# Attention in a fused kernel: two units of one kind per turn of the loop

## The chip, the core and the metric

The kernel runs on one core of a Trainium2 chip. The metric is the time of one execution on the device in microseconds, lower is better. The engines named below are TensorE (PE, with its weight loads as PEld), VectorE (DVE), ScalarE (ACT), GpSimd (POOL) and SyncE (SP, which here only issues DMAs). Each engine works through its own list of instructions in order and waits on semaphores for results of the others.

## The reference

Four batches, eight heads, 576 positions, 64 features per head; 2304 tokens of 512 features; float32 in and out.

```python
scores = scale * q @ k.T                          # per batch and head, 576 x 576
rel = pos[:, None] - pos[None, :]
mask = (rel >= 0) & (rel < 32)                    # heads 0 to 3 (local)
mask = (rel >= 0) & same remainder modulo 32      # heads 4 to 7 (strided)
attn = softmax(where(mask, scores, -1e9)) @ v
x = attn as [2304, 512]
e = argmax(x @ w_gate + modality_bias[modality_id], 1)    # one of 8 experts per token
x = gate * (relu(x @ w1[e]) @ w2[e])
out = relu(x @ w_in) ** 2 @ w_out
```

## The kernel before

The program has three stages: attention with the gate's logits, the routing (sorting tokens by expert), and the two feed-forward layers. Only the first is touched.

Attention is cut into units. Of the local heads there are 18 units (kind "l"): 128 queries of four heads, each half of 64 queries against 96 keys. Of the strided heads there are 22 units (kind "s"): positions are regrouped by remainder modulo 32, a unit holds six remainders of 18 positions each, in two groups of 54, and the last unit is shorter. `units` (lines 116 to 126) lists ten s units, then s and l by turns, then the last seven l units: 40 units, and one turn of the loop (lines 427 to 455) starts one of them. The tiles are written in program order and each engine's list is that order.

A unit goes through these steps. `stage_s` (L182): PE writes the mask into PSUM tile `sp` through an identity matmul (L194) and adds the score products (L206); filler matmuls on `warm` (L192, counts in `KEEP0` and `KEEP`) stand ahead of them. `v_max` and `v_sub` (L215, L221): DVE takes the row maximum and the difference, ACT the exponential into `sm`. `stage_t` (L230): PE transposes the weights into `pp`, ACT copies them to `pt`. `stage_v` (L243): PE multiplies with v into `xp`; a column of ones in v gives the row sums. `norm` (L421): DVE adds 1e-9 (L274), takes the reciprocal (L279) and multiplies into `xn` (L284). `features` and `stage_x` (L379, L314): PE transposes `xn` into `xq`, ACT copies it into `xT`, and for tokens whose features are complete PE forms the product with the gate's weights (`products`, L359), ACT copies it (`fetch`, L364), and one turn later PE folds its four parts (`folds`, L370) into `sp` and DVE adds the bias (`add`, L591).

The distances are in the line

```python
LT, LV, LN, LX = 2, 3, 4, 5
```

so that in turn k the scores of unit k, the transposes of unit k-2, the products with v of unit k-3, the normalisation of unit k-4 and the features of unit k-5 are issued. `pp`, `xp` and `xq` have one PSUM buffer each, `sp` has two. Loads of q, k and v come through SP in groups of one or two units into rings of `NLD` = 7 buffers; `xn` is stored by POOL with a delay of up to `DEFER` units. Behind the loop a tail (L469 to L514) drains the units still under way and then calls the routing (`finish`), whose first counting matmul is L628.

Of the kernel before, what the change touches and what calls it, by code (L numbers as in the profile page):

```python
# [43 lines left out]
DEFER = 16  # L44
# [4 lines left out]
KEEP0 = {0: 0, 1: 4, 2: 4, 3: 4, 4: 4, 5: 4, 6: 3, 7: 3, 8: 3, 9: 2, 10: 2}  # L49
S_FIRST = 10  # L50
L_LAST = 7
# [31 lines left out]
def attention_and_routing(es, tc, a, x1, res):  # L83
# [32 lines left out]
    units = []  # L116
    ns, nl = S_FIRST, 0
    units += [("s", t) for t in range(ns)]
    while ns < NST or nl < NTL - L_LAST:
        if nl < NTL - L_LAST and (ns == NST or nl * (NST - S_FIRST) <= (ns - S_FIRST) * (NTL - L_LAST)):  # L120
            units.append(("l", nl))
            nl += 1
        else:
            units.append(("s", ns))
            ns += 1
    units += [("l", t) for t in range(nl, NTL)]
    NU = len(units)
# [41 lines left out]

    def geom(k):  # L170
        kind, t = units[k]
        gi, o = gof[kind, t]
        if kind == "s":
            return kind, t, 128 if t < NST - 1 else 64, 64, gi, o
        return kind, t, 128, 96, gi, o

    st = {}
# [3 lines left out]

    def stage_s(k):  # L182
        kind, t, n, w, gi, o = geom(k)
        sp = ps.tile([128, 2, 512], F32, tag="sp", name="sp")
        qk = qk_t[gi]
        if kind == "s":
            mk = mstr
        else:
            mk = mloc[:, 1 if (2 * t) % 9 == 0 else (2 if (2 * t + 1) % 9 == 0 else 0), :]
        mk = mk.unsqueeze(1).to_broadcast([128, 2, w])  # L190
        for i in range(KEEP0.get(k, KEEP[kind])):
            pe.matmul(sp[:, i % 2, 256:512], lhsT=warm[:, 0:128], rhs=warm[:, 0:256], start=True, stop=True)  # L192
        for par in range(2):
            pe.matmul(sp[:, par, 0:2 * w].rearrange("p (b w) -> p b w", b=2),  # L194
                      lhsT=identb, rhs=mk, start=True, stop=False, skip_group_check=True)
        for pr in range(2):
            for par in range(2):
                r0 = 64 * par
                if kind == "s":
                    cq, ck = (4 * o + pr) * SU, (4 * o + 2 + pr) * SU  # L200
                    blocks = [(g, cq + g * SR, m, ck + g * SR, m) for g, m in sgroups(t)]
                else:
                    cq, ck = o * QL + 128 * pr, o * QL + 256 + 160 * pr
                    blocks = [(e, cq + 64 * e, 64, ck + 64 * e, 96) for e in range(2)]
                for g, cq, m, ck, mk_ in blocks:
                    pe.matmul(  # L206
                        sp[64 * g:64 * g + m, par, pr * w:pr * w + mk_],
                        lhsT=qk[r0:r0 + 64, cq:cq + m],
                        rhs=qk[r0:r0 + 64, ck:ck + mk_],
                        start=False, stop=True, skip_group_check=True,  # L210
                    )
        st[k, "s"] = sp[0:n, :, 0:2 * w].rearrange("p a (b w) -> p a b w", b=2)
        return sp

    def v_max(k):  # L215
        kind, t, n, w, gi, o = geom(k)
        mx = wk.tile([128, 2, 2], F32, tag="mx", name="mx")
        ve.tensor_reduce(out=mx[0:n], in_=st[k, "s"], axis=AX.X, op=ALU.max)
        st[k, "m"] = mx

    def v_sub(k):  # L221
        kind, t, n, w, gi, o = geom(k)
        sm = wk.tile([128, 4 * w], F32, tag="sm" + kind, name="sm")
        sm4 = sm.rearrange("p (a b w) -> p a b w", a=2, b=2)[0:n]
        ve.tensor_tensor(out=sm4, in0=st.pop((k, "s")),
                         in1=st.pop((k, "m"))[0:n].unsqueeze(3).to_broadcast([n, 2, 2, w]), op=ALU.subtract)
        ac.activation(out=sm[0:n], in_=sm[0:n], func=AF.Exp, scale=scale)
        st[k, "p"] = sm

    def stage_t(k, pp=None):  # L230
        kind, t, n, w, gi, o = geom(k)
        p = st.pop((k, "p"))
# [5 lines left out]
        ac.activation(  # L238
            out=pt[0:c, 0:nb, 0:n], in_=pp.rearrange("p (h n) -> p h n", h=4)[0:c, 0:nb, 0:n], func=AF.Copy
        )  # L240
        st[k, "t"] = pt

    def stage_v(k, xp=None):  # L243
        kind, t, n, w, gi, o = geom(k)
        pt = st.pop((k, "t"))
        v = v_t[gi]
        if kind == "s":
            xp = ps.tile([128, 2, 512], F32, tag="xp", name="xp", bufs=1)
            for par in range(2):
                for pr in range(2):  # L250
                    for g, m in sgroups(t):
                        p0 = 64 * pr
                        pe.matmul(  # L253
                            xp[64 * g:64 * g + 64, pr, 66 * par:66 * par + 65],
                            lhsT=pt[p0:p0 + m, par, 64 * g:64 * g + 64], rhs=v[p0:p0 + m, o, 2 * g + par, 0:65],
                            start=True, stop=True,
                        )
            st[k, "v"] = xp[0:n, :, 0:132].rearrange("p a (b c) -> p a b c", b=2)
            return
        xp = bank("xp") if xp is None else xp  # L260
        for i in range(4):
            h = 2 * (i % 2) + i // 2
            for e in range(2):
                pe.matmul(  # L264
                    xp[64 * e:64 * e + 64, 66 * h:66 * h + 65],
                    lhsT=pt[0:96, i, 64 * e:64 * e + 64], rhs=v[0:96, 2 * o + e, h, 0:65],
                    start=True, stop=True,
                )
        st[k, "v"] = xp[:, 0:264].rearrange("p (a b c) -> p a b c", a=2, b=2)

    def v_norm1(k):
        n = geom(k)[2]
        rs = wk.tile([128, 2, 2, 1], F32, tag="rs", name="rs")
        ve.tensor_scalar(out=rs[0:n], in0=st[k, "v"][:, :, :, 64:65], scalar1=1e-9, scalar2=None, op0=ALU.add)  # L274
        st[k, "r"] = rs

    def v_norm2(k):
        n = geom(k)[2]
        ve.reciprocal(out=st[k, "r"][0:n], in_=st[k, "r"][0:n])  # L279

    def v_norm3(k):
        kind, t, n, w, gi, o = geom(k)
        xn = wk.tile([128, 256], F32, tag="xn", name="xn", bufs=DEFER + 4)
        ve.tensor_tensor(  # L284
            out=xn[0:n].rearrange("p (a b d) -> p a b d", a=2, b=2), in0=st.pop((k, "v"))[:, :, :, 0:64],
# [135 lines left out]
    def norm(u):  # L421
        v_norm1(u)
        v_norm2(u)
        v_norm3(u)
# [1326 lines left out]
```

## Time and profile before

| | us |
|---|---|
| median of 3 timed runs | 743.71 (742.12 to 744.97) |
| profiled execution | 749.47 |
| its span, first to last instruction | 747.7 |
| PE busy in it | 722.5 |
| DVE busy | 521.5 |
| ACT busy | 413.0 |
| mean granted TensorE clock | 0.974 |

Busy times are sums over the whole span; what bounds one stage is read from the waits inside that stage. In the rows further below, a line of the timeline gives the start, the duration and, in brackets, the idle time of that engine before it with the instruction or transfer that ended it. "issue" is time in which an engine waited for nothing that the profile shows. PEclk is the granted clock as a share of full speed.

### The profile page before, as it was taken

The numbers are of one execution on the slowest core, as the hardware profiler recorded it, in microseconds if no ns is written. First come the engines' busy times: TensorE is split into PE (matmuls) and PEld (weight loads), VectorE is DVE, ScalarE is ACT, GpSimd is POOL, SyncE is SP. The second block draws the span as 40 slices with busy tenths as digits, with TensorE's granted clock in tenths as the row PEclk, the third lists the DMA queues.
The fourth block names the chain that finished last, engine by engine and source line by source line (L and its number), as shares of the span: only waits on it lengthen the run. The fifth ranks groups of instructions, "written<-read, shape, count | busy, mean of one in ns | idle before, by whom it ended". The sixth has DMA issues, their size and how long they took to land.

```text
span 747.7 us, 14684 instructions
## 1 busy us (share of the span) xinstructions
PE 722.5 (97%) x5520; PEld 668.4 (89%) x5522; DVE 521.5 (70%) x1025; ACT 413.0 (55%) x797; POOL 161.3 (22%) x232
## 2 busy tenths in 40 slices
PE   8999998999999999999999999999999999999994
PEld 5767674889999998999999999989999999999994
DVE  4857666458877778777457799846746796774682
ACT  3645454445455547644456677657636746654750
POOL 7543223110331044003001444540000004000003
PEclk8979899899999999999999999999999999999998
DMA  7999313556686579648036799998888879887812
GB/s 213 276 267 264 96 53 128 183 178 208 227 288 224 188 243 322 227 147 291 10 126 184 253 318 352 350 326 257 254 251 243 251 240 321 251 250 247 256 59 85
DMA packets 67168, 166.48 MB, mean 223 GB/s; under 512 B 10962, under 2 KB 12194, under 8 KB 67094
## 3 DMA queue, kind: packets, MB, share of 16 engines
q1 hardware_dynamic: 50198, 121.42, 52.5%
q0 software_dynamic: 16896, 44.09, 16.5%
q8 instruction: 45, 0.74, 0.4%
q14 instruction: 29, 0.24, 0.1%
HBM read 126.64 MB, written 38.80 MB: 221 GB/s over the span
## 4 chain that ended last, share of the span: by engine, by line
PE 91%; DMA 3%; DVE 2%; issue 1%; ACT 1%; POOL 1%; SPq 0%; POOLq 0%; ACTq 0%; DVEq 0%
PE hp L874 14%; PE yp L885 13%; PE fhp L1144 9%; PE op L1165 9%; PE mb L1518 7%; PE lb L1456 7%; PE md L1518 5%; PE ma L1518 5%; PE md L1456 4%; PE la L1456 4%; PE sp L206 2%; PE pp L236 2%; PE xq L318 2%; PE xp L264 1%; PE xp L253 1%
## 5 line engine op out<-in xcount | busy, mean ns | idle before, releaser
L874 PE MATMUL hp<-xh,w 128*128 128x384 f32 (+1 forms) x448 | 94.0, 333 | 2.7 <-DVE hl L879 1.4
L840 ACT ACTIVATE w<-stg 128x1024 fp32r<-128x1024 f32 x56 | 59.3, 1060 | 66.8 <-PE yp L885 42.2
L844 DVE TENSOR_TENSOR w<-stg,w 128x1024 fp32r<-128x1024 f32 x56 | 68.3, 1222 | 38.5 <-ACT w L840 37.5
L874 PEld LDWEIGHTS hp<-xh,w 128*128 128x128 f32 x448 | 78.2, 192 | 5.2 <-ACT w L840 2.1
L885 PE MATMUL yp<-hh,w 128*128 128x384 f32 x384 | 76.2, 340 | 0.0
L1144 PE MATMUL fhp<-xh,w 128*128 128x384 f32 x256 | 70.5, 336 | 0.0
L885 PEld LDWEIGHTS yp<-hh,w 128*128 128x128 f32 x384 | 66.9, 188 | 0.0
L1172 POOL DMA_INDIRECT out_dram<-x2t,idn x12 | 12.7, 1058 | 225.0 <-DVE x2t L1431 223.1
L1456 PE MATMUL lb<-xh,ws 128*128 128x384 f32 x192 | 55.1, 338 | 0.7 <-ACT ob L1402 0.7
L1190 POOL DMA_DIRECT2D wd<-w x48 | 34.5, 900 | 90.2 <-DVE w L995 86.5
L1165 PE MATMUL op<-w,gh 128*128 128x512 f32 x192 | 49.1, 391 | 0.0
L1505 DVE TENSOR_TENSOR gl<-g,gh 128x384 fp32r<-128x384 f32 x64 | 33.6, 554 | 21.7 <-ACT gh L1504 21.7
L1144 PEld LDWEIGHTS fhp<-xh,w 128*128 128x128 f32 x256 | 46.7, 188 | 1.2
L874 PE MATMUL hp<-xl,w 128*128 128x384 f32 (+1 forms) x224 | 47.0, 331 | 0.0
L1144 PE MATMUL fhp<-xl,w 128*128 128x384 f32 x128 | 43.2, 338 | 0.0
L877 ACT ACTIVATE hh<-hp 128x384 fp32r<-128x384 f32 (+1 forms) x56 | 25.5, 456 | 31.7 <-PE hp L874 30.8
L1434 ACT ACTIVATE g<-g 128x384 f32<-128x384 f32 x48 | 25.1, 522 | 32.0 <-DVE g L1431 31.8
L1518 PE MATMUL mb<-ws,gh 128*128 128x256 f32 x288 | 42.1, 282 | 0.4 <-ACT gh L1504 0.4
L1504 ACT ACTIVATE gh<-g 128x384 fp32r<-128x384 f32 x64 | 32.5, 522 | 16.4 <-PE mb L1518 8.7
L885 PE MATMUL yp<-hl,w 128*128 128x384 f32 x192 | 41.1, 336 | 0.0
L1165 PEld LDWEIGHTS op<-w,gh 128*128 128x128 f32 x192 | 35.6, 188 | 5.4
L874 PEld LDWEIGHTS hp<-xl,w 128*128 128x128 f32 x224 | 39.7, 191 | 0.0
(291 smaller groups left out, 1769.8 us busy)
## 6 DMA issues: line engine op xcount, KB each, us to landing
ws<-wd SPq DMA_DIRECT2D x112, 512.0 KB
stg<-in_wcat_dram SPq DMA_DIRECT2D x56, 512.0 KB
stg<-in_w2cat_dram SPq DMA_DIRECT2D x32, 512.0 KB
wd<-w POOLq DMA_DIRECT2D x48, 256.0 KB
wd<-co POOLq DMA_DIRECT2D x16, 512.0 KB
wd<-co POOLq DMA_DIRECT2D x32, 256.0 KB
qk<-in_qkl_dram SPq DMA_DIRECT2D x9, 576.0 KB
qk<-in_qks_dram SPq DMA_DIRECT2D x9, 432.0 KB
```

The lines of the kernel that those rows point to most:

```text
L840: ac.activation(out=w[:, 0, :], in_=t, func=AF.Copy)
L844: ve.tensor_tensor(out=w[:, 1, :], in0=t, in1=w[:, 0, :].bitcast(F32), op=ALU.subtract)
L874: pe.matmul(hp, lhsT=w[:, wi, 128 * k:128 * k + 128], rhs=x[:, k, 0:n], start=(i == 0), stop=(i == 11))
L877: ac.activation(out=hh, in_=hp, func=AF.Relu)
L885: pe.matmul(yp[c][:, 0:SLOT], lhsT=w[:, wi, 512 + 128 * c:640 + 128 * c], rhs=x, start=(j == 0 and x is hh and wi == 0), stop=(j == NC1 - ...
L1144: pe.matmul(hp, lhsT=w[:, v, 128 * k:128 * k + 128], rhs=xs[ch, k // 2][xv][:, k % 2, :], start=(i == 0), stop=(i == 11))
L1165: pe.matmul(ops[ch][t], lhsT=x[:, 128 * t:128 * t + 128], rhs=w[:, v, :], start=(j == ORD[0] and first), stop=(j == ORD[-1] and last))
L1190: gp.dma_start(out=wd[lay, p // 4, 7 * (p % 4) + unit[lay][i]], in_=src)
L1456: pe.matmul(M[m], lhsT=w[:, v, k, :], rhs=xp_c[c][x][xv][:, k, :], start=(i < 3 and n == 0), stop=(n == 5), skip_group_check=True)
L1504: ac.activation(out=gh, in_=src, func=AF.Copy)
L1505: ve.tensor_tensor(out=gl, in0=src, in1=gh.bitcast(F32), op=ALU.subtract)
L1518: pe.matmul(M2[m][:, 256 * t:256 * t + 256], lhsT=x[:, 128 * t:128 * t + 128], rhs=w[:, v], start=(new and e == 0 and x is gh and v == 0 a ...
```

## The change

A turn now takes a pair: two s units or two l units. The list of turns has five s pairs, then l and s pairs by turns, then two l pairs and the last two l units alone: 21 turns instead of 40. In a turn, mask, maximum, difference, exponential, reciprocal and normalising product are one instruction for both units (for l pairs with different masks, the mask stays one instruction per unit and half). For s pairs the two transposes per unit become four in one `pp` and one copy; for l pairs `pp` is filled and copied once per unit. In turn k the scores of pair k, the transposes and the products with v of pair k-1, and the normalisation and features of pair k-2 are issued; the constants LT to LX go. The feature copies of the first unit of a pair move to DVE (for s units one of their two halves). `xn` has 12 buffers of two units instead of 20 of one, `DEFER` is 18 instead of 16, and the filler counts are given per pair. The tail is rewritten for what is left under way.

```diff
--- before
+++ after
-DEFER = 16
+DEFER = 18
 KEEP_D = 2
 NOH = (3, 7)
 QL = 2 * 128 + 2 * 160
 KEEP = {"s": 1, "l": 0}
-KEEP0 = {0: 0, 1: 4, 2: 4, 3: 4, 4: 4, 5: 4, 6: 3, 7: 3, 8: 3, 9: 2, 10: 2}
-S_FIRST = 10
-L_LAST = 7
+KEEP0 = {0: 0, 1: 8, 2: 8, 3: 6, 4: 5, 5: 3}
+S_FIRST = 5
+L_LAST = 4
...
+    sp_, lp_ = [[2 * i, 2 * i + 1] for i in range(NST // 2)], [[2 * i, 2 * i + 1] for i in range(NTL // 2 - 1)]
+    lp_ += [[NTL - 2], [NTL - 1]]
+    NSP, NLP = len(sp_), len(lp_)
...
+        if kind == "s":
+            masks = [(mstr, 0, 2 * nu)]
+        else:
+            masks = [(mloc[:, first(t), :], 2 * u, 2) for u, t in enumerate(ts)]
+            if len({first(t) for t in ts}) == 1:
+                masks = [(masks[0][0], 0, 2 * nu)]
         for par in range(2):
+            for mk, b0, nb in masks:
+                pe.matmul(sp[:, par, b0 * w:(b0 + nb) * w].rearrange("p (b w) -> p b w", b=nb),
+                          lhsT=identb, rhs=mk.unsqueeze(1).to_broadcast([128, nb, w]),
+                          start=b0 == 0, stop=False, skip_group_check=True)
...
+    def v_max(k):
+        kind, ts, nu, w = geom(k)
+        mx = wk.tile([128, 2, 2 * nu], F32, tag="mx", name="mx", padded_shape=[128, 2, 4])
+        ve.tensor_reduce(out=mx, in_=st[k, "s"], axis=AX.X, op=ALU.max)
+        st[k, "m"] = mx
+
+    def v_sub(k):
+        kind, ts, nu, w = geom(k)
+        sm = wk.tile([128, 4 * nu * w], F32, tag="sm", name="sm", padded_shape=[128, 768], bufs=2)
+        sm4 = sm.rearrange("p (a b w) -> p a b w", a=2, w=w)
+        ve.tensor_tensor(out=sm4, in0=st.pop((k, "s")),
+                         in1=st.pop((k, "m")).unsqueeze(3).to_broadcast([128, 2, 2 * nu, w]), op=ALU.subtract)
+        ac.activation(out=sm, in_=sm, func=AF.Exp, scale=scale)
+        st[k, "p"] = sm
+
+    def stage_t(k, part, pp=None):
+        kind, ts, nu, w = geom(k)
+        if part >= (1 if kind == "s" else nu):
+            return
+        p = st[k, "p"].rearrange("p (a c) -> p a c", a=2)
+        pp = bank("pp") if pp is None else pp
+        pt = wk.tile([128, 4, 128], F32, tag="pt", name="pt")
+        if kind == "s":
+            n, c = 2 * nu, 128
+            cols = [p[:, i // nu, 128 * (i % nu):128 * (i % nu) + 128] for i in range(n)]
+        else:
+            n, c = 4, 96
+            cols = [p[:, i // 2, 192 * part + 96 * (i % 2):192 * part + 96 * (i % 2) + 96] for i in range(n)]
+        for i, col in enumerate(cols):
+            pe.transpose(pp[0:c, 128 * i:128 * i + 128], col, ident)
+        ac.activation(out=pt[0:c, 0:n], in_=pp.rearrange("p (h n) -> p h n", h=4)[0:c, 0:n], func=AF.Copy)
+        st[k, "t", part] = pt
...
-    def stage_t(k, pp=None):
-        pp = bank("pp") if pp is None else pp
-        nb, c = (2, 128) if kind == "s" else (4, 96)
-        for i in range(nb):
-            pe.transpose(pp[0:c, 128 * i:128 * i + n], p[0:n, c * i:c * i + c], ident[0:n, 0:n])
-        pt = wk.tile([128, 4, 128], F32, tag="pt", name="pt")
-        ac.activation(
-            out=pt[0:c, 0:nb, 0:n], in_=pp.rearrange("p (h n) -> p h n", h=4)[0:c, 0:nb, 0:n], func=AF.Copy
-        )
-        st[k, "t"] = pt
-
...
+        xn = wk.tile([128, nu, 256], F32, tag="xn", name="xn", bufs=DEFER // 2 + 3, padded_shape=[128, 2, 256])
...
-                ac.activation(out=tok.rearrange("p (g m) j -> p g m j", g=2),
-                              in_=src[:, c].rearrange("p (g x) -> p g x", g=2)[:, :, 0:SR]
-                              .rearrange("p g (m j) -> p g m j", j=NJ), func=AF.Copy)
+                move(on_ve and c == 1, tok.rearrange("p (g m) j -> p g m j", g=2),
+                     src[:, c].rearrange("p (g x) -> p g x", g=2)[:, :, 0:SR]
+                     .rearrange("p g (m j) -> p g m j", j=NJ))
...
+        stage_x(k, u, xq, VEX[u])
...
-    LT, LV, LN, LX = 2, 3, 4, 5
+    VEX = (True, False)
...
-    loc = 0
-    for k in range(NU):
-        if k >= LN:
-            norm(k - LN)
-        while len(stores) > max(1, min(DEFER, DEFER + 20 - k)):
+    loc, nst = 0, 0
+    for k in range(NP):
+        kind, ts, nu, w = geom(k)
+        if k >= 2:
+            norm(k - 2)
+        nst += nu
+        while len(stores) > max(1, min(DEFER, DEFER + 20 - nst)):
             store()
         side(1)
-        loads_to(geom(k)[4] + NLD - 1)
+        loads_to(gof[kind, ts[-1]][0] + NLD - 1)
         sp = stage_s(k)
-        fd = folds(lt_p.pop(0), sp[:, 0, 192:256]) if lt_p else None
+        fd = []
+        while lt_p:
+            i = len(fd)
+            fd.append(folds(lt_p.pop(0), sp[:, 0, 448 + 16 * i:464 + 16 * i]))
         v_max(k)
-        if fd:
-            add(fd)
+        for f in fd:
+            add(f)
         side(1)
-        if k >= LX:
-            features(k - LX)
-        if k >= LT:
-            stage_t(k - LT)
+        if k >= 2:
+            features(k - 2, 0)
+        if k >= 1:
+            stage_t(k - 1, 0)
         side(1)
         v_sub(k)
-        side(1)
-        if k >= LV:
-            stage_v(k - LV)
-        if k == 3:
+        if k >= 2:
+            features(k - 2, 1)
+        if k >= 1:
+            stage_t(k - 1, 1)
+        side(2)
+        if k >= 1:
+            stage_v(k - 1)
...
-    norm(L - 3)
+    norm(L - 1)
...
-    stage_t(L - 1, bank("a0"))
-    stage_x(L - 4, bank("xq"), True)
-    stage_v(L - 2, bank("a1"))
-    stage_t(L, bank("pp"))
...
+    stage_t(L, 0, bank("a0"))
...
+    stage_x(L - 1, 0, bank("xq"), True)
+    xp = bank("xp").unsqueeze(1)
+    stage_v(L, xp)
+    norm(L)
...
+    stage_x(L, 0, bank("b1"))
...
```

ACT's list in the middle of the loop, before: one s unit and the l unit behind it. `sm` is the exponential, `pt` the copy of the transposed weights, `xT` the copy of the features, `lt` the copy of the gate's product.

```order
L331 ACTIVATE xT<-xq 128x6x18 [waits PE_49]
L331 ACTIVATE xT<-xq 128x6x18
L364 ACTIVATE lt<-xq 128x128
L238 ACTIVATE pt<-pp 96x512 [waits PE_49,Activation_49]
L227 ACTIVATE sm<-sm 128x384 [waits DVE_49]
L295 ACTIVATE xT<-xq 128x2x128 [waits PE_49]
L238 ACTIVATE pt<-pp 128x256 [waits PE_49,Activation_49]
L227 ACTIVATE sm<-sm 128x256 [waits DVE_49]
```

The same place after: a turn with an s pair's scores, then the start of one with an l pair's.

```order
L318 ACTIVATE xT<-xq 128x6x18 [waits PE_49]
L384 ACTIVATE lt<-xq 128x128 [waits DVE_49]
L253 ACTIVATE pt<-pp 96x512 [waits PE_49,Activation_49]
L235 ACTIVATE sm<-sm 128x512 [waits DVE_49,Activation_49]
L318 ACTIVATE xT<-xq 128x6x18 [waits PE_49]
L318 ACTIVATE xT<-xq 128x6x18
L253 ACTIVATE pt<-pp 96x512 [waits PE_49,Activation_49]
L253 ACTIVATE pt<-pp 128x512 [waits PE_49,Activation_49]
L235 ACTIVATE sm<-sm 128x768 [waits DVE_49,Activation_49]
```

Before, every `pt` copy stands ahead of the exponential of its turn; after, the second `pt` copy of an l pair stands behind it. PE's list at the same place, before: an s unit's scores to the next mask.

```order
L206 MATMUL sp<-qk 54x54 x8
L370 MATMUL sp<-fold,lt 128x8 [waits Activation_49]
L318 MATMUL xq<-ident,xn 128x128 [waits PE_49]
L318 MATMUL xq<-ident,xn 128x128
L236 MATMUL pp<-ident,sm 128x128 [waits Activation_49]
L236 MATMUL pp<-ident,sm 128x128
L264 MATMUL xp<-v,pt 64x65 [waits DVE_49,PE_49]
L264 MATMUL xp<-v,pt 64x65 x7
```

PE after, from the gate's product in an s pair's turn to the second xp of the l pair before it.

```order
L379 MATMUL xq<-xT,wg 32x128 [waits PE_49]
L379 MATMUL xq<-xT,wg 32x128 x3
L341 MATMUL xq<-ident,xn 128x128 [waits DVE_49]
L341 MATMUL xq<-ident,xn 128x128
L252 MATMUL pp<-ident,sm 96x128 x4
L341 MATMUL xq<-ident,xn 128x128 [waits Activation_49]
L341 MATMUL xq<-ident,xn 128x128
L252 MATMUL pp<-ident,sm 96x128 [waits Activation_49]
L252 MATMUL pp<-ident,sm 96x128 x3
L279 MATMUL xp<-v,pt 64x65 [waits DMAHW7_49]
L279 MATMUL xp<-v,pt 64x65 x7
L279 MATMUL xp<-v,pt 64x65 [waits Activation_49]
```

PE now asks ACT three times between its scores and the end of the turn: for the `xq` buffer, for the `pp` buffer and for the second `pt`.

## Rows read from the trace of the kernel before

**Rows 1.** Page, chain that ended last: shares of the span by engine.
```profile
PE 91%; DMA 3%; DVE 2%; issue 1%; ACT 1%; POOL 1%; SPq 0%; POOLq 0%; ACTq 0%; DVEq 0%
```
**Rows 2.** Timeline, PE, one round: start us, duration us, instructions [idle before].
```profile
62.41 0.34 PE L194 MATMUL sp<-mloc,identb 128*128 128x192 bf16 x2
...
63.16 0.43 PE L359 MATMUL xq<-xT,wg 128*32 128x128 f32 x8
63.52 0.44 PE L318 MATMUL xq<-ident,xn 128*128 128x128 f32 x2
63.80 0.60 PE L236 MATMUL pp<-ident,sm 128*96 128x128 f32 x4
64.33 0.46 PE L253 MATMUL xp<-v,pt 54*64 54x65 f32 x16
64.72 0.28 PE L192 MATMUL sp<-warm 128*128 128x256 bf16 x1
...
65.05 0.42 PE L206 MATMUL sp<-qk 64*54 64x54 f32 x16
65.40 0.39 PE L370 MATMUL sp<-fold,lt 128*128 128x8 f32 x2
65.64 0.42 PE L318 MATMUL xq<-ident,xn 128*128 128x128 f32 x2
...
66.21 0.69 PE L264 MATMUL xp<-v,pt 96*64 96x65 f32 x16
66.83 0.34 PE L194 MATMUL sp<-mloc,identb 128*128 128x192 bf16 x2
```
**Rows 3.** Chain in order of time, first 80 us: start us, us, what.
```profile
12.27 0.63 PE sp L206 x16
...
43.33 1.30 issue
...
74.93 1.67 issue
```
**Rows 4.** Windows: from:to, us, busy us (instructions) of each engine, PEclk, DMA, GB/s.
```profile
58.90:67.70 8.80, 8.80 (x180) 6.52 (x176) 7.00 (x23) 5.23 (x16) 3.65 (x6) 1.00 1.04 280
46.00:56.30 10.30, 10.30 (x126) 7.29 (x126) 4.92 (x16) 4.38 (x13) 4.23 (x7) 0.51 1.02 279
76.80:83.60 6.80, 6.80 (x79) 4.82 (x73) 2.89 (x9) 2.42 (x8) 0.59 (x1) 0.50 0.42 124
```
**Rows 5.** Groups by shape, 0 to 113 us: busy us, mean ns | idle before.
```profile
L218 DVE TENSOR_REDUCE mx<-sp 128x4 f32<-128x384 f32 x18 | 10.0, 557 | 1.8 <-PE sp L206 0.9 <-PE sp L370 0.7
...
L227 ACT ACTIVATE sm<-sm 128x256 f32<-128x256 f32 x21 | 8.7, 414 | 5.8 <-DVE sm L225 5.5
```
**Rows 6.** Timeline, DVE and ACT in the round of rows 2.
```profile
64.00 0.55 ACT L331 ACTIVATE xT<-xq 128x108 f32<-128x108 f32 x2 [1.19 <-PE xq L318]
...
64.55 0.58 ACT L238 ACTIVATE pt<-pp 96x512 f32<-96x512 f32 x1
...
64.86 0.16 DVE L274 TENSOR_SCALAR rs<-xp 128x4 f32<-128x4 f32 x1 [0.34 <-PE xp L253]
...
65.01 0.52 ACT L227 ACTIVATE sm<-sm 128x384 f32<-128x384 f32 x1
...
65.27 0.42 DVE L284 TENSOR_TENSOR xn<-xp,rs 128x256 f32<-128x256 f32 x1
...
65.83 0.42 DVE L218 TENSOR_REDUCE mx<-sp 128x4 f32<-128x256 f32 x1
```
**Rows 7.** Timeline, end of the attention loop and the tail.
```profile
87.82 0.34 PE L194 MATMUL sp<-mloc,identb 128*128 128x192 bf16 x2
...
102.27 0.64 PE L236 MATMUL a<-ident,sm 128*96 128x128 f32 x4
...
111.26 0.18 DVE L591 TENSOR_TENSOR lg<-xq,mb 128x24 f32<-128x24 f32 x1 [0.23 <-PE xq L370]
...
112.79 0.18 PE L628 MATMUL xp<-cbc,oh 128*128 128x2 bf16 x1
```

More of the change, by code (lines that the diff above doesn't have):

```diff
@@ L168, in loads_to, with first @@
             ngl[0] += 1
+    st = {}
     def geom(k):
[L171 to L177, printed above, removed]
+        kind, ts = pairs[k]
+        return kind, ts, len(ts), 64 if kind == "s" else 96
     def sgroups(t):
         return [(g, min(SR, NT - t * SU - g * SR)) for g in range(2) if t * SU + g * SR < NT]
+    def first(t):
+        return 1 if (2 * t) % 9 == 0 else (2 if (2 * t + 1) % 9 == 0 else 0)
@@ L196, in stage_s @@
[L196 to L210, printed above, removed]
-                    )
@@ new lines, in stage_s @@
+        for u, t in enumerate(ts):
+            gi, o = gof[kind, t]
+            qk = qk_t[gi]
+            for pr in range(2):
+                for par in range(2):
+                    r0 = 64 * par
+                    if kind == "s":
+                        cq, ck = (4 * o + pr) * SU, (4 * o + 2 + pr) * SU
+                        blocks = [(g, cq + g * SR, SR, ck + g * SR, SR) for g in range(2)]
+                    else:
+                        cq, ck = o * QL + 128 * pr, o * QL + 256 + 160 * pr
+                        blocks = [(e, cq + 64 * e, 64, ck + 64 * e, 96) for e in range(2)]
+                    for g, cq, m, ck, mk_ in blocks:
+                        pe.matmul(
+                            sp[64 * g:64 * g + m, par, (2 * u + pr) * w:(2 * u + pr) * w + mk_],
+                            lhsT=qk[r0:r0 + 64, cq:cq + m],
+                            rhs=qk[r0:r0 + 64, ck:ck + mk_],
+                            start=False, stop=True, skip_group_check=True,
+                        )
@@ new lines, in norm @@
+    def norm(k):
+        kind, ts, nu, w = geom(k)
+        xp = st.pop((k, "v"))
+        xn = wk.tile([128, nu, 256], F32, tag="xn", name="xn", bufs=DEFER // 2 + 3, padded_shape=[128, 2, 256])
+        if kind == "s":
+            xv = xp[:, :, 0:132 * nu].rearrange("p a (b c) -> p a b c", c=66)
+            parts = [(xn[:, u].rearrange("p (a b d) -> p a b d", a=2, b=2), u) for u in range(nu)]
+            sh = [128, 2, 2 * nu, 1]
+        else:
+            xv = xp[:, 0:nu, 0:264].rearrange("p a (b c) -> p a b c", c=66)
+            sh = [128, nu, 4, 1]
+        rs = wk.tile(sh, F32, tag="rs", name="rs", padded_shape=[128, 2, 4, 1])
+        ve.tensor_scalar(out=rs, in0=xv[:, :, :, 64:65], scalar1=1e-9, scalar2=None, op0=ALU.add)
+        ve.reciprocal(out=rs, in_=rs)
+        if kind == "s":
+            rd = rs.rearrange("p a (u b) o -> p a u b o", u=nu)
+            ve.tensor_tensor(
+                out=xn.rearrange("p u (a b d) -> p a u b d", a=2, b=2),
+                in0=xv[:, :, :, 0:64].rearrange("p a (u b) d -> p a u b d", u=nu),
+                in1=rd.to_broadcast([128, 2, nu, 2, 64]), op=ALU.mult,
+            )
+        else:
+            ve.tensor_tensor(out=xn.rearrange("p u (h d) -> p u h d", h=4), in0=xv[:, :, :, 0:64],
+                             in1=rs.to_broadcast([128, nu, 4, 64]), op=ALU.mult)
+        for u, t in enumerate(ts):
+            stores.append((kind, t, xn[:, u]))
@@ L299, in store @@
     def store():
-        k, xn = stores.pop(0)
-        kind, t = geom(k)[0:2]
+        kind, t, xn = stores.pop(0)
         if kind == "l":
@@ L345, in attention_and_routing, with lg_ready @@
     lg_done = [0]
-    def lg_ready(k):
-        done = set(units[:k])
+    def lg_ready(done):
         n = lg_done[0]
```

181 lines of the change are left out of this document (68 added, 113 removed).

## The prediction

> **What bounds the kernel now.** I read the chain that ended last first: 91% of the span is TensorE (PE) [rows 1]. So only what PE does, or what it waits for, can move the time. The change ends with the routing, so only the first 113 us matter; the stages behind it start from the routing's result and shift as a block. Next I read one round of the attention loop at full clock in order of time: an l unit and an s unit (l: neighbouring keys, s: every 32nd key). The PE groups start one behind the other from 62.41 to 66.83 without a hole, 4.42 us for two units [rows 2]. In the same round DVE and ACT are done with each result before PE asks for it, since transposes, products with v and normalisation run two, three and four units behind the scores. The loop is bound by PE's issue, and four units cost 2 x 4.42 = 8.84 us.
>
> Two other things cost time before the routing. PE stands 1.30 us and 1.67 us with nothing that the profile can name, and at 12.27 us it starts on data that came late [rows 3]. Behind the first of these stalls the granted clock is 0.51, near the lower of the two levels (1.2 of 2.4 GHz), from 46.0 to 56.3 us [rows 4]. In that stretch PE does 126 instructions in 10.3 us, where the full-clock stretch does 180 in 8.8 us [rows 4]. 126 instructions would take 6.2 us there, so the low stretch costs about 4.1 us. The one behind the second stall (79 instructions in 6.8 us [rows 4]) costs 2.9 us by the same division.
>
> **The change, part by part.** A turn now handles two units of one kind. I call it an S turn where the scores of an s pair are made (and the products with v of the l pair before it), and an L turn the other way round.
>
> *What goes away.* PE's work is the same but for masks, filler matmuls and folds. One s unit takes 0.33 us for filler and mask and 0.35 us for its scores [rows 2]; a pair takes 0.70 us for scores, and filler and wider mask lie between 0.33 and 0.66: I take 0.45, the nearer end. An l unit takes 0.75 us for mask and scores [rows 2]; a pair lies between 1.24 and 1.50: 1.43. With one fold (0.24), one product with the gate (0.36), two xq transposes (0.28 each), the pp transposes (0.53 per l unit) and xp (0.62 per l unit, 0.39 per s unit) [rows 2], an S turn is 0.45+0.70+0.24+0.36+0.56+1.06+1.24 = 4.61 us of PE and an L turn 1.43+0.24+0.36+0.56+0.53+0.78 = 3.90 us: 8.51 for four units, 0.33 less than now.
>
> On DVE, a maximum of 256 takes 0.42 us and one of 384 takes 0.56 [rows 5, 6]: 0.13 us per 128 elements and 0.15 fixed, so 512 is about 0.70 and 768 about 0.98. Difference and normalising product run at the same rate. On ACT, an exponential of 256 takes 0.41 and of 384 takes 0.52 [rows 5, 6], so 512 is 0.62 and 768 is 0.83. Five fixed parts of about 0.15 us per pair go on DVE, but DVE is not the bound, so this alone is worth nothing.
>
> *What comes on the path.* The distances shrink. Transposes and products with v now belong to the pair just before, in the same turn, and ACT copies pt between them. ACT takes its work in the written order, and there the second pt copy of an l pair stands behind the exponential of the turn, which needs this turn's scores, maximum and difference. The S turn, from PE's start at 0:
> - The normalisation begins 0.14 after PE issued its last xp (64.72 to 64.86), its product 0.41 later at 0.55 [rows 2, 6], and for 512 elements it ends at 1.25.
> - PE: filler, mask, scores to 1.15, fold to 1.39, gate product to 1.75, xq to 2.03, pp to 2.56. The maximum starts 0.19 after the fold (65.64 to 65.83) [rows 2, 6]: 1.58 to 2.28; the logit sum follows to 2.41.
> - The first xq copy starts on ACT 0.20 after PE left it (63.80 to 64.00) [rows 2, 6], at 2.23, and ends at 2.60. The other half is now DVE's, and waits for ACT's: about 2.65 to 2.91. Then the difference, 2.90 to 3.60, and the exponential from 3.63.
> - ACT can start something 0.46 after a 512 copy started (64.55 to 65.01) [rows 6]: at 4.09 the two copies of the second unit's features (0.17 each), at 4.43 the second pt copy, done at 5.02. PE's last xp runs from 5.07 to 5.69.
>
> So PE stands about 1.1 us of this turn, and it lasts 5.7 us. The L turn: scores to 1.43, fold to 1.67, maximum of 768 from 1.86 to 2.84, sum to 2.97, DVE's copy of 256 (0.42) to 3.37. The gate product waits for this copy: 3.42 to 3.78, then xq to 4.06 and xp of the s pair to 4.84. That is 4.85 us, with about 0.9 us standing. A round is 10.55 us against 8.84: **+1.7 us, six rounds, +10.2 us**. If every wait were hidden it would be 8.51: -0.33 a round, -2.0 in all; if nothing overlapped better than I laid out and the masks cost their upper end, +2.0 a round, +12.
>
> *The last six l units.* Now they take 87.82 to 102.27, 14.45 us [rows 7]. An L turn after an L turn makes both long chains one: difference to 4.33, exponential from 4.36, the second unit's copy and the logit copy until 5.5, pt to 6.1, xp to 6.8 us. The four turns are 4.85 (still behind s), 6.8, about 5.1 (one unit behind a pair, maximum and difference of 384) and about 3.7 (one unit behind one): 20.45 us, **+6.0 us**; bounds -0.4 (PE's work alone) and +8.
>
> *The tail.* From 102.27 to the first counting matmul at 112.79 is 10.5 us [rows 7], with three units to drain. Now one and a half remain: pp 0.53, pt copy 0.2+0.59, xp 0.62, normalisation 0.97, xq 0.48, copy 0.43, logits 0.25, and then the last logit sum and the block of small DVE work behind it, which takes 1.53 now (111.26 to 112.79 [rows 7]) and has one more such block ahead of it that I put at 0.6 (it lies partly beside the normalisation). That is 6.2 us: **-4.3 us**, bounds -6 and -2.
>
> *The start.* The same bytes come in the same order, so the late data at 12.27 [rows 3] stays. PE fills up to eight matmuls ahead of it now, and the turns behind it have only s units: between -2 and +1, I take **-0.5 us**.
>
> *Stalls.* The 1.30 and 1.67 us [rows 3] may recur, since PE's program is only 6% shorter. In a turn with 0.9 to 1.1 us of standing, part of such a stall falls into time already lost: **-1.0 us** for both, bounds -3 and 0. Low-clock stretches are taken as before.
>
> *Moved without a price.* Stores may now hang back by 18 units instead of 16. POOL alone issues them and no one waits for POOL in this stretch; were they late, the normalising product would wait for a free xn buffer, 24 units deep now against 20, so I cost it at nothing. The loads keep SP's order and distance, and a slower loop cannot make them late.
>
> Sum: 10.2 + 6.0 - 4.3 - 0.5 - 1.0 = **+10.4 us**. The profiled execution took 749.47 us (span 747.7), so it would be about 759.9; the median of the timed runs is 743.71, 5.8 us less, and the step is added to that: 754.1 us. I say **753.5 us**, since DVE operations start a little before the one ahead has ended (0.07 us) and I gave nothing for that.
>
> **Rivals.** *Hidden after all (faster).* If ACT and DVE ran ahead so far that the second pt copy was ready when PE came to the second xp, the round would be PE's 8.51 us: -2.0 for six rounds, -0.4 at the end, -4.3 in the tail, -0.5 at the start: -7.2, 736.5 us. For it speaks that the tail really is shorter; against it, that the exponential ahead of the copy needs scores of the same turn. It decides from the point where norm, maximum, difference, exponential and copy together fit in 4.6 us of PE; I count 5.0 up to the end of the copy. Chance 0.10.
>
> *No stalls, no low clock (no change).* The filler in turns 1 to 3 closes the first hole, and the two stalls may fall where PE stands. Then the low stretches of 4.1 and 2.9 us go, and the 2 us of stalls still in the sum: 753.5 - 9.0 = 744.5 us. For it speaks that both low stretches came behind a stall; against, that PE's program and the loads keep their size. Chance 0.18.
>
> *More low clock (slower still).* PE now stands in every turn, some 20% of the round. If these holes bring the clock down as the stalls did, half of a loop of 84 us (six rounds of 10.55 and the last 20) at the low level costs 42 x 4.1/10.3 = 17 us more: 770 us. Against it: the holes of one turn are each shorter than either stall. Chance 0.15.
>
> The full-clock stretch has no hole and the low one follows a hole [rows 3, 4]. The Trainium skill, "TensorE: Matmul & The Clock Gate", section "A second HAM failure mode: psum-queue depth-cycling", says that PE idling briefly and often between groups of matmuls is enough to make its clock go back and forth. By that rule this third rival would be the likely one, at about 770 us; the trace has no stretch with many short holes to show it, so I leave it at its chance.
>
> **How the numbers follow.** The forecast itself holds 0.57, and its own range, from the bounds of its terms, is 748 to 758. A measurement of this kernel can tell about 0.5%, 3.7 us, from no change: faster is below 740.0, slower above 747.4. Faster takes the first rival, 0.10. The same takes most of the second and a little of the forecast: 0.17. Slower is the rest, 0.73. The range reaches down into the second rival, to 743, and up towards the third, to 763; it leaves out the first rival and the upper part of the third.
>
> **What would show it.** In the profile after, PE rows of the middle turns should have holes, released by ACT's pt copy (in S turns) and DVE's xT copy (in L turns); four units should take about 10.5 us at full clock; the last four turns about 20 us; the tail about 6 us. I am wrong if PE groups still follow each other without holes, or if the stretch up to the first counting matmul is not longer than 113 us.

## The result: slower by 1.1%

The changed kernel takes 750.95 us (749.02 to 752.79), the kernel before 742.91 beside it; the ratio is 1.0114 [1.0072, 1.0155] (here and below, the brackets are a 95% interval). In the experiments below the medians are over all executions, while the ratios leave out those over 1.5% above their kernel's fastest, so the two can differ.

The profiled execution of the kernel before behind [rows 1 to 7] was a long one (749.47 us), so the kernel before was run and profiled again: 739.88 us, span 738.1. That trace stands against the one of the changed kernel (749.02 us, span 747.2) from here on. First PE's own rows of the kernel before, repeated: the first l unit's mask, four stalls, the mask of the last six l units, the end of the loop, the first counting matmul.

```profile
23.00 0.33 PE L194 MATMUL sp<-mloc,identb 128*128 128x192 bf16 x2
...
27.36 0.42 PE L206 MATMUL sp<-qk 64*54 64x54 f32 x16 [2.23 <-DMA qk<-in_qks_dram]
...
63.80 0.41 PE L359 MATMUL xq<-xT,wg 128*32 128x128 f32 x4 [1.08 <-issue]
...
71.00 0.32 PE L206 MATMUL sp<-qk 64*54 64x54 f32 x7 [0.56 <-issue]
...
78.33 0.32 PE L206 MATMUL sp<-qk 64*64 64x96 f32 x2 [0.51 <-issue]
...
80.14 0.34 PE L194 MATMUL sp<-mloc,identb 128*128 128x192 bf16 x2
...
94.58 0.64 PE L236 MATMUL a<-ident,sm 128*96 128x128 f32 x4
...
106.30 0.21 PE L628 MATMUL xp<-cbc,oh 128*128 128x2 bf16 x1
```

The same places in the changed kernel:

```profile
23.64 0.49 PE L198 MATMUL sp<-mloc,identb 128*128 128x192 bf16 x4
...
29.53 0.30 PE L214 MATMUL sp<-qk 64*54 64x54 f32 x2 [1.21 <-issue]
...
84.15 0.50 PE L198 MATMUL sp<-mloc,identb 128*128 128x192 bf16 x4
...
103.98 0.64 PE L252 MATMUL a<-ident,sm 128*96 128x128 f32 x4
```

The counting matmul follows at 114.51 us. The difference of the spans, 9.1 us, comes out as:

| stretch | before, repeated | after | difference |
|---|---|---|---|
| up to the first l mask | 23.00 | 23.64 | +0.6 |
| six rounds of four units | 57.14 | 60.51 | +3.4 |
| last six l units | 14.44 | 19.83 | +5.4 |
| tail, to the counting matmul | 11.72 | 10.53 | -1.2 |
| behind it | 631.80 | 632.69 | +0.9 |

PE does the same work in the six rounds, but no longer without holes: one window of each trace (columns as in [rows 4]), the kernel before first.

```profile
22.90:80.10 57.20, 52.81 (x1028) 38.71 (x1026) 41.52 (x128) 30.81 (x99) 26.65 (x44) 0.97 1.00 265
```

```profile
23.60:84.10 60.50, 50.11 (x1024) 36.09 (x1022) 35.53 (x83) 26.57 (x68) 26.58 (x44) 1.00 0.94 256
107.40:114.50 7.10, 6.22 (x23) 3.63 (x23) 3.10 (x16) 1.02 (x4) 0.55 (x1) 0.52 0.07 22
```

PE was busy 52.8 of 57.2 us and is now busy 50.1 of 60.5. One round in order of time shows where it stands; this answers [rows 2, 6].

```profile
53.58 0.50 PE L198 MATMUL sp<-mloc,identb 128*128 128x384 bf16 x2
...
55.26 0.96 DVE L226 TENSOR_REDUCE mx<-sp 128x8 f32<-128x768 f32 x1 [0.43 <-PE sp L390]
...
56.20 0.41 DVE L316 COPY xT<-xq 128x256 f32<-128x256 f32 x1
...
56.67 0.43 PE L379 MATMUL xq<-xT,wg 128*32 128x128 f32 x8 [0.74 <-DVE xT L316]
...
58.02 0.28 PE L189 MATMUL sp<-warm 128*128 128x256 bf16 x1
...
60.15 0.36 ACT L318 ACTIVATE xT<-xq 128x108 f32<-128x108 f32 x1 [1.29 <-PE xq L341]
...
60.54 0.34 DVE L316 COPY xT<-xq 128x108 f32<-128x108 f32 x1 [0.35 <-ACT xT L318]
...
60.91 0.28 ACT L384 ACTIVATE lt<-xq 128x128 f32<-128x128 f32 x1 [0.40 <-DVE xT L316]
...
61.24 0.44 PE L341 MATMUL xq<-ident,xn 128*128 128x128 f32 x2 [0.69 <-ACT lt L384]
...
61.56 0.63 ACT L235 ACTIVATE sm<-sm 128x512 f32<-128x512 f32 x1
...
62.30 1.50 PE L279 MATMUL xp<-v,pt 96*64 96x65 f32 x32
...
62.46 0.59 ACT L253 ACTIVATE pt<-pp 96x512 f32<-96x512 f32 x1
...
63.73 0.50 PE L198 MATMUL sp<-mloc,identb 128*128 128x192 bf16 x4
```

An L turn from 53.58 to 58.02 (4.44 us) and an S turn from 58.02 to 63.73 (5.71). The round is 10.15 against 8.84 in [rows 2]. In the L turn PE's gate product waits 0.74 us for DVE's feature copy, which stands behind the maximum of 768. In the S turn PE's second xq transposes wait 0.69 us for ACT's lt copy. Behind them the second pt copy (62.46, behind the exponential at 61.56) is done at 63.05, and the 32 xp matmuls take 1.43 us where two l units take 2 x 0.62 [rows 2], so that this one costs 0.19. Up to 120 us, PE's waits (us in total, times, longest):

```profile
PE xq L379 <- DVE xT L316: 4.4, 6, 0.9
PE xq L341 <- ACT lt L384: 4.0, 6, 0.7
...
PE xq L341 <- DVE xT L316: 1.7, 4, 0.5
...
PE xp L279 <- ACT pt L253: 0.9, 2, 0.6
PE xp L269 <- ACT pt L253: 0.7, 1, 0.7
```

DVE's copy of 60.54 starts when ACT's is done, and ACT's lt copy when DVE's is done, though all three only read the same xq buffer. The Trainium skill, "PSUM — Partial Sum Buffer", section "PSUM bank collisions raise a hardware error", says that the compiler back end's scheduler puts an order between instructions of different engines on the same bank and the same 32 partitions, reads against reads too. The trace agrees: the three copies stand one behind the other, with 0.03 us between each end and the next start. So the copy that was moved to DVE does not run beside ACT's; it adds two handovers to the chain.

The tail in the changed kernel, which answers [rows 7]:

```profile
106.56 0.42 DVE L308 TENSOR_TENSOR xn<-xp,rs 128x256 f32<-128x256 f32 x1
...
107.39 0.47 PE L390 MATMUL xr<-fold,lt 128*128 128x8 f32 x2
...
107.96 0.28 ACT L384 ACTIVATE lt<-a 128x128 f32<-128x128 f32 x1 [2.70 <-PE xr L390]
...
109.06 0.67 PE L341 MATMUL b<-ident,xn 128*128 128x128 f32 x2
...
111.71 2.96 PE L634 MATMUL a<-warm 128*128 128x512 bf16 x7
...
112.29 0.23 DVE L623 TENSOR_TENSOR oh<-eq,m 128x16 bf16<-128x16 f32 x1
...
114.51 0.17 PE L642 MATMUL xp<-cbc,oh 128*128 128x2 bf16 x1
```

### The profile page after: what moved, and what is told of

Read it like the earlier page. It is cut to its first block, busy times and chain, and to the rows that moved or that the text cites. A ratio compares the mean times of both kernels' runs of the same rounds, so it can differ in the third digit from the quotient of the medians.

```text
span 747.2 us, 14483 instructions
## 1 busy us (share of the span) xinstructions
PE 709.7 (95%) x5521; PEld 657.7 (88%) x5521; DVE 513.0 (69%) x953; ACT 404.3 (54%) x748; POOL 161.2 (22%) x232
## 3 DMA queue, kind: packets, MB, share of 16 engines
q1 hardware_dynamic: 50198, 121.42, 52.8%
## 4 chain that ended last, share of the span: by engine, by line
PE 75%; DMA 2%; DVE 2%; ACT 1%; issue 1%; POOL 0%; SPq 0%; ACTq 0%; POOLq 0%; DVEq 0%
PE hp L888 13%; PE yp L899 12%; PE fhp L1158 9%; PE op L1179 9%; PE mb L1532 7%; PE lb L1470 7%; PE md L1532 5%; PE ma L1532 5%; PE md L1470 4%; PE la L1470 4%; DMA stg<-in_wcat_dram 2%; PE tp L877 1%; ACT w L854 1%; DVE w L858 1%; DMA stg<-in_w2cat_dram 1%
## 5 line engine op out<-in xcount | busy, mean ns | idle before, releaser
L888 PEld LDWEIGHTS hp<-xh,w 128*128 128x128 f32 x448 | 76.4, 188 | 5.7 <-ACT w L854 2.9
```

Source lines behind the costliest of these rows:

```text
L888: pe.matmul(hp, lhsT=w[:, wi, 128 * k:128 * k + 128], rhs=x[:, k, 0:n], start=(i == 0), stop=(i == 11))
```

## Experiments

Each version ran beside the kernel before. The time is the median; the ratio is to the kernel before beside it.

**Kernel before, repeated.** No edit.

> The kernel before, unchanged, for a second profile. In the first one PE lost two named stalls and three low-clock stretches before the routing's first counting matmul at 112.8 us, and its time of 749.5 us stood 6 us above the timed runs. If the change's loss of about 8 us is a longer loop, this profile should have the counting matmul at about 105 to 107 us where the clock stayed up, against 114.5 us in the changed kernel. If the changed kernel lost its time somewhere behind the routing, the matmul stays near 112 us.

742.58 us, ratio 0.9992 [0.9959, 1.0025]. The counting matmul stands at 106.30, as expected; the 8.2 us from there to 114.51 are nearly all of the 9.1.

**Short distances with single units.** The changed code with one unit per "pair", all feature copies on ACT, and the unit order, filler counts and buffer depths of before:

```diff
-    sp_, lp_ = [[2 * i, 2 * i + 1] for i in range(NST // 2)], ...
+    sp_, lp_ = [[i] for i in range(NST)], [[i] for i in range(NTL)]
-    VEX = (True, False)
+    VEX = (False, False)
```

> The changed kernel's short distances without its pairs: every turn is one unit again, transposes and products with v are of the unit just before, features two turns back, and all feature copies are on ACT. Theory 1 (the short distance costs the time): PE waits in each turn for the pt copy, 0.2 plus 0.4 to 0.6 us, for some 30 units, so 755 to 768 us, worse than the pairs. Theory 2 (the long instructions of a pair cost the time, not the distance): about 743 us, as before. Theory 3 (the feature copy on DVE costs it): about 743 us too, since that copy is not on DVE here.

778.0 us, ratio 1.0440 [1.0365, 1.0515]: the direction of theory 1, and more than its 755 to 768 us; theories 2 and 3 expected no change. PE waits 25.7 us for pt, and the profiled span (766.3) is 28.2 us longer than that of the kernel before, repeated:

```profile
PE xp L278 <- ACT pt L252: 13.0, 17, 1.0
PE xp L268 <- ACT pt L252: 12.7, 22, 0.8
```

Two units take 5.95 us against 4.42 [rows 2]. By the ratios, the short distance with single units costs nearly four times what the change costs. So handling two units at once is not the cause: with the same distances and copies it loses 0.7% (next experiment) where single units lose 4.4%. That one chain of waits is then paid for two units is the likely reason, not shown by itself.

**All feature copies on ACT.**

```diff
-    VEX = (True, False)
+    VEX = (False, False)
```

> The changed kernel with all feature copies on ACT, as before the change. In its profile PE waits 0.69 us in each S turn for the logit copy, which waits for DVE's feature copy, and 0.74 us in each L turn for that copy itself. Theory 3 (this copy behind the maximum on DVE is what holds PE): both waits go, six rounds of 1.4 us less some new waiting, 742 to 746 us. Theory 1 (the distance): the same turn still needs pt behind its exponential, so the waits move to the second xp and little is won, 748 to 751 us.

746.64 us, ratio 1.0074 [1.0037, 1.0110]; the round falls from 10.15 to 9.40.

```profile
PE xq L341 <- ACT lt L384: 1.8, 6, 0.3
...
PE xq L379 <- ACT xT L318: 1.1, 1, 1.1
PE sp L390 <- ACT lt L384: 1.1, 4, 0.3
...
PE xq L341 <- ACT xT L318: 0.9, 5, 0.2
```

The waits for lt and xT fall from 10.1 us to 4.9, and those for pt do not grow (1.7 us after 1.6), though PE comes earlier. That fits a difference on DVE that no longer stands behind a copy. The time lies between what theories 3 and 1 expect, nearer to theory 3.

**Longer distances.** Products with v one turn later, normalisation and features three turns behind, buffers to match, one more pair to drain:

```diff
-        if k >= 2:
-            norm(k - 2)
+        if k >= 3:
+            norm(k - 3)
...
-        if k >= 1:
-            stage_v(k - 1)
+        if k >= 2:
+            stage_v(k - 2)
```

> Pairs as in the changed kernel, but the products with v one turn later and with them normalisation and features, so that no pt copy is asked for in its own turn; the feature copy of the first unit stays on DVE; the logit copies get five buffers. Theory 1 (the distance of the products with v): the wait of the second xp goes in every turn, 743 to 746 us. Theory 3 (DVE's feature copy): the gate product and the xq transposes still wait 0.7 us in each turn, 748 to 751 us.

750.34 us, ratio 1.0092 [1.0057, 1.0127]; the round is 9.30. No wait for pt is left in the loop. Those for DVE's copy, and for the lt copy behind it, stay in part (the first of DVE's was 4.4 us in the changed kernel):

```profile
PE xq L341 <- ACT lt L384: 4.2, 6, 0.8
...
PE xq L379 <- DVE xT L316: 2.3, 5, 0.9
```

The time gains nothing, so theory 1's 743 to 746 us failed: the longer drain ran at the low clock (0.51) from 99.7 to 120.2, and the counting matmul stands at 114.67.

**Longer distances and all copies on ACT.** The two edits above together.

> The kernel with the longer distances (products with v one turn later, normalisation and features three turns behind), with both feature copies on ACT. Theory 1 (distance and DVE's copy each make their own holes, and together they are the whole loss of the loop): the round of two turns falls from 10.15 us in the changed kernel (9.30 with distance alone, 9.40 with the copies alone) to 8.5 to 8.9, the 8.84 of the kernel before, and the loop ends 3 us earlier than in the run with distance alone; the drain of one more pair stays, so the time is 745 to 748 us. Theory 2 (the holes left are the logit copies, which the pairs put into one bunch whatever the distance): the round stays at 9.2 or more, and the time at 749 to 751 us.

749.79 us, ratio 1.0099 [1.0065, 1.0132]. The maxima of two l pairs in turn:

```profile
52.07 0.96 DVE L226 TENSOR_REDUCE mx<-sp 128x8 f32<-128x768 f32 x1 [0.87 <-PE sp L390]
...
60.85 0.96 DVE L226 TENSOR_REDUCE mx<-sp 128x8 f32<-128x768 f32 x1 [0.45 <-PE sp L390]
```

The round is 8.78, and 8.67 two rounds on: the 8.84 of before is back. The round between them takes 9.82, with a stall of PE of 1.02 us in it. For the round, the two causes are thus shown: distance alone back, 9.30; copies alone back, 9.40; both, 8.78. The time does not follow, though: theory 1's round held and its 745 to 748 us failed. The profile shows where the gain went. The six rounds take 52.57 us, 4.6 less than in the kernel before, repeated (stalls included in both), but the last six l units with the longer drain take 22.35 instead of 14.44, and PE comes to the first l mask 2.1 us later.

**Four lt buffers.** `bufs=2` becomes `bufs=4`.

> The changed kernel with four buffers for the logit copies lt in place of two, so that the third copy of the tail (at 107.96 us in the changed kernel, 2.70 us after ACT was free) does not wait for PE's folds. Theory A (the tail's missing 4.3 us are a serial chain: lt copy, fold, add, fold, with the last xq transposes behind it): the third copy starts by 105.6, PE's last xq transposes start 1 us or more earlier against the last normalising product, and the tail from the last pp transposes (103.98) to the counting matmul (114.51) shrinks from 10.5 to about 9.0: 749.5 us. Theory B (what delays the xq transposes is DVE, whose logit sums stand behind the last normalisation, so that the folds wait for DVE in any case): the copy is early, the folds are not, and the time stays within 0.5 us of the changed kernel, 750 to 752 us.

750.21 us, ratio 1.0089 [1.0058, 1.0120].

```profile
104.62 0.27 ACT L384 ACTIVATE lt<-a 128x128 f32<-128x128 f32 x1
...
106.80 0.37 PE L390 MATMUL xr<-fold,lt 128*128 128x8 f32 x2
```

The lt copy comes at once, but the folds keep their place behind PE's logits, and the tail is 10.37 instead of 10.53: theory B's number, with PE's order and not DVE's as the reason for the first fold. The rounds stay at 10.15 us, so the further lt buffers are not what shortens the round in the runs with longer distances. One round is longer, and it has a stall of PE in its S turn:

```profile
58.30 0.30 PE L214 MATMUL sp<-qk 64*54 64x54 f32 x3 [0.72 <-issue]
```

From one maximum of 768 to the next (53.77 to 64.94) it takes 11.17 us instead of 10.15, at a clock of 1.00, and PE's usual waits of 0.7 us for DVE's xT copy and for ACT's lt copy stand in it as in the others: the stall is ahead of the chain and delays it too.

**Two fillers ahead of the counting matmul.** `KEEP_R = (7, 9, 12)` becomes `(2, 9, 12)`.

> The changed kernel with two filler matmuls of 512 columns in place of seven ahead of the first counting matmul. In the changed kernel the one-hot of the logits is ready at 112.52, but PE comes to the counting matmul only at 114.51, after seven fillers that took 2.96 us at the low granted clock. Theory A (these fillers are on the path, since the clock is low there): the counting matmul comes 1.9 us earlier against the last logits, and the time falls by 1.5 to 2 us: 749 us. Theory B (the fillers hold the clock up for the stages behind): the stretch behind the counting matmul, 632.7 us in the changed kernel, becomes longer by 1 us or more, and the time stays at 750 to 753 us.

749.60 us, ratio 1.0092 [1.0059, 1.0125]. In its profile the tail is 7.52 us (106.02 to 113.54) instead of 10.53, and the stretch behind stays at 632.7: theory A in the trace.

```profile
106.00:112.60 6.60, 5.62 (x61) 4.33 (x58) 3.89 (x17) 1.57 (x5) 1.09 (x2) 1.00 0.13 43
...
113.25 0.23 DVE L623 TENSOR_TENSOR oh<-eq,m 128x16 bf16<-128x16 f32 x1
...
113.54 0.19 PE L642 MATMUL xp<-cbc,oh 128*128 128x2 bf16 x1 [0.29 <-DVE oh L623]
```

The fillers are not all of these 3.0 us. Up to them PE's list is the changed kernel's, and the first fold stands 3.42 us into the tail (3.41 there), but here the clock is 1.00 up to 112.60, where the changed kernel has 0.52 from 107.40 on. From that fold to the one-hot it takes 4.04 us instead of 5.13: 1.1 us go with the clock, and 1.9 with the fillers behind the one-hot. The time moved by less than the interval can tell.

**Copies on ACT, four lt buffers, two fillers.**

> All copies on ACT (746.64 us before), four buffers for the logit copies, and two fillers in place of seven ahead of the counting matmul. If the loss in the tail is what theories A of the two runs on the tail say, it is 1.5 us of folds and 1.8 us of fillers shorter: 743.5 us, the time of the kernel before. If neither is on the path, 746 to 747 us.

749.98 us, ratio 1.0098 [1.0063, 1.0132]: no gain over the copies alone, and neither expectation (743.5, or 746 to 747) held. Its tail is 7.83 us (102.55 to 110.38), but behind the counting matmul it takes 638.6 instead of 632.7.

**Tail in another order.** Loop unchanged; four lt buffers, two fillers, and:

```diff
+    stage_x(L, 0, bank("b1"))
     lf = bank("xr")
-    while lt_p:
-        add(folds(lt_p.pop(0), lf))
-        lf = bank("pp")
-    stage_x(L, 0, bank("b1"))
+    fd = [folds(p, lf[:, 16 * i:16 * i + 16]) for i, p in enumerate(lt_p)]
+    lt_p.clear()
+    for f in fd:
+        add(f)
```

> The changed kernel with its loop untouched and the tail rewritten: the last xq transposes stand ahead of the folds on PE, the folds go to columns of one bank and none waits for a logit sum, lt has four buffers, and two fillers stand ahead of the counting matmul in place of seven. Theory A (the tail's 10.5 us in place of the predicted 6.2 is the folds and fillers on PE, 2.0 us each): from the last pp transposes to the counting matmul it is 6 to 7 us in the trace, and the time is about 747 us. Theory C (the tail is bound by DVE's small blocks whatever PE does): 8 us or more.

749.56 us, ratio 1.0096 [1.0059, 1.0134].

```profile
102.71 0.64 PE L252 MATMUL a<-ident,sm 128*96 128x128 f32 x4
...
110.05 0.19 PE L643 MATMUL xp<-cbc,oh 128*128 128x2 bf16 x1 [1.76 <-DVE oh L624]
```

The tail is 7.34 us, between what theories A and C expect, and the time misses A's 747. Against the run with two fillers, whose tail also ran at the full clock nearly to its end, this is 0.2 us less. So the place of the folds was worth little; fillers and low clock were worth the 3.0 above. The counting matmul comes 4.5 us earlier than in the changed kernel, yet the span is only 1.2 us shorter. Two windows of this trace:

```profile
109.70:116.00 6.30, 5.80 (x18) 2.34 (x19) 5.80 (x26) 3.24 (x9) 2.43 (x3) 0.50 0.00 0
129.90:136.70 6.80, 5.87 (x19) 5.47 (x20) 3.74 (x5) 2.04 (x3) 1.59 (x2) 0.50 0.62 183
```

The clock is low for 6.3 us right behind the counting matmul, and later for 6.8. In the changed kernel those stretches were 7.1 us inside the tail (the window from 107.40 above) and 3.9 later.

**The same tail with all copies on ACT, and with longer distances as well.**

> The same tail with all copies on ACT in the loop. If both savings add up: the loop is 4 us shorter than in the changed kernel and the tail 3.5 to 4 us, 742.5 to 744 us. If a shorter routing is given back in lower granted clock behind it, as the mean clock of 0.982 over the runs with copies on ACT and two fillers suggests (0.987 in the changed kernel), 746 to 749 us with a mean clock of 0.983 or less.

> The same tail with the longer distances and all copies on ACT. Its loop has the round of the kernel before (about 8.8 us), so what is left above the kernel before is one more pair to drain and the start: 743 to 745 us if nothing is given back, 746 to 748 us if the clock is (mean granted clock 0.983 or less).

745.53 us, ratio 1.0034 [0.9999, 1.0069], and 748.33 us, ratio 1.0077 [1.0039, 1.0114]. The counting matmul stands at 107.16 and 107.24, but the stretches behind take 634.8 and 638.4. The mean granted clock over the compared runs is 0.985 and 0.981, against 0.987 in the changed kernel. The first time lies between the two expectations, the second just above the one for a gain given back.

**The kernel before with two fillers.**

> The kernel before with two fillers in place of seven ahead of the counting matmul. In its repeated run the one-hot is ready at 105.05 and the counting matmul starts at 106.30: 1.0 us earlier, 741.5 to 742 us, if the clock is low there; no difference where it is full, since seven fillers then end with the one-hot. Either way not to be told from the kernel before by the time alone; if the fillers keep the clock up for what follows, it is slower, 744 us or more.

744.01 us, ratio 1.0014 [0.9977, 1.0050]: no difference that can be told, as expected of the time alone. Its counting matmul stands at 104.73 instead of 106.30, its stretch behind takes 635.4 instead of 631.8.

No version beats the kernel before. The best with pairs is the one with the new tail and all copies on ACT, at 1.0034.

Where the gains of the later versions went is seen in the profiles, not separated by an experiment: what is won in the loop and the tail is partly lost to the low clock behind the counting matmul. Why the low stretches come there more often in these profiles stays open.

## Why the prediction was right, point by point

The sum was right (750.95 in a range of 743 to 763, direction and size), and the loop's mechanism is shown. That the number came so close is partly luck: against the repeated trace, rounds and stalls came out 5.9 us below their terms, the tail 3.1 above, the start and the stretch behind together 2.0 above, and these largely cancelled.

- **S turn: right.** 5.7 us predicted, 5.71 measured; second pt copy from 4.43 to 5.02 predicted, 4.44 to 5.03 measured. But the step put the standing into one hole in front of the last xp. Most of it lies at the second xq transposes (0.69 against 0.19). Both hang on the same chain: DVE's copy delays lt as well as the difference, and through that the exponential and pt.
- **L turn: right, 0.4 too long.** The hole is where it was put (gate product behind DVE's xT copy). Mask and scores took 1.25 us up to the fold, not 1.43, with one mask instruction per half for both units (53.58) as with one per unit (63.73).
- **Six rounds:** +1.31 each in the middle of the loop (10.15 against 8.84) instead of +1.7. With the stalls (below) taken out, all six take 59.30 us against 52.76, since the first ones are shorter: +6.5 instead of +10.2.
- **Last six l units:** +5.4 instead of +6.0.
- **Stalls: the size was off, and the reason failed.** -1.0 predicted. The kernel before, repeated, lost 4.4 us to stalls in its rounds (2.23, 1.08, 0.56 and 0.51 above; [rows 3] has others); the changed kernel shows one, 1.21 us at 29.53: -3.2. The prediction's reason was that part of a stall falls into time already lost. But the stall in the run with four lt buffers, where PE works through the same list, made its round longer by 1.0 us, and the first round took 10.11 us with its 1.21 us in the changed kernel and 9.37 with a stall of 0.46 in that run: the whole stall counts. So the holes took nothing in. There were fewer stalls in this one execution, which is luck as far as the runs show. The second rival, given 0.18, had that outcome in part, but not its reason. Its 744.5 us also takes the low stretches of one long execution off a median: in the repeated profile the counting matmul came 6.5 us earlier with no change at all. And PE's matmuls up to the counting matmul are 1758 and 1756 in the two traces, not 6% fewer.
- **Tail: failed.** 6.2 us predicted, 10.5 measured. The step priced the last units' chain and gave nothing for what stands in PE's list between its links, and it took the clock as before. The seven fillers take 2.96 us at a clock of 0.52, and behind them the counting matmul came 2.0 us after its one-hot was ready at 112.52. By the run with two fillers, the fillers are 1.9 of the 4.3 us missing and the low clock ahead of them 1.1. The two more folds behind logit sums look costly (normalised at 106.98, transposed only at 109.06), but moving them won 0.2 us. The last 1.1 us are not separated.
- **Start:** -0.5 predicted, +0.6 measured, inside its bounds.
- **The third rival** did not come: with a hole in every turn PE's clock is 1.00 over the 60.5 us of the six rounds. The Trainium skill, "TensorE: Matmul & The Clock Gate", section "A second HAM failure mode: psum-queue depth-cycling", reports a kernel whose clock goes up and down because PE idles briefly and often between groups of matmuls. The trace here does not agree: holes of some 0.7 us in every turn, 17% of the stretch in all, did not bring the clock down. The low clock came in the tail, where PE waits on DVE and ACT in a chain.
- **Hidden after all** did not come: the round shows holes.

## What to carry to other kernels

Making instructions wider and fewer on an engine that is not the bound won nothing by itself here (a round of 8.78 us against 8.84 once distances and copies were as before); look at what the regrouping does to the distance between producer and consumer. Here the short distance cost 1.5 us for every two single units and 0.6 us for every four in pairs, with all copies on ACT; with part of them on DVE it was 1.3 us for every four. Before a copy is moved to an idle engine, see who else reads that buffer. And of a drain, price every instruction in the bound engine's list between the links of the chain, fillers first, and at the clock that the drain gets.

## What was not expected of the hardware

In these runs a microsecond saved ahead of the low-clock stretches was not kept whole. The kernel with all copies on ACT, four lt buffers and two fillers reached its counting matmul 4.1 us before the changed kernel and was 1.0 us faster; its mean granted clock over the runs was 0.982 against 0.987 (the kernel before beside it: 0.988). The link to the earlier routing is not strict: with the longer distances alone the counting matmul was no earlier, and the clock was 0.983. The profile of the first kernel also has a low stretch far behind the routing (0.62 from 291 to 300 us), and so has the run with four lt buffers, whose counting matmul stands at 113.76.

The stalls that the profile names no reason for often come at the same place of PE's list and differ in length: ahead of the last seven score products of one s unit in the two profiles of the kernel before and the one of its version with two fillers (1.67, 0.56 and 0.84 us), and ahead of the last two of the first S turn in four profiles with the changed kernel's loop (1.21, 0.46, 1.64 and 0.27). Other profiles with the same order on PE have none there.
